# Adding two of the three patterns of a score group in SBUF with an accumulating DMA

## The chip, the cores and the metric

The kernel runs on one core of a Trainium2 chip. The metric is the device time of one execution in microseconds (us), as a median over runs. TensorE multiplies matrices into PSUM, VectorE and ScalarE read PSUM and write SBUF, GpSimd (Pool in the profile) works on SBUF alone and issues DMAs of its own, and SyncE (SP) issues most of the DMAs.

## The reference

Two attention blocks read the same input x of 2048 rows and 512 columns, with 32 heads of 16 columns each. A gate of x mixes their outputs. Block B is the softmax attention with 2048 x 2048 scores per head, and it is most of the work.

```
def _A_ref(x, wqkv, w_phi, wo):          # linear attention
    ...
    phi_q = concatenate([_softmax(pq), _softmax(-pq)])   # same for phi_k
    kv = einsum("bhsf,bhsd->bhfd", phi_k, v);  z = einsum("bhsf->bhf", phi_k)
    o = einsum("bhqf,bhfd->bhqd", phi_q, kv) / (einsum("bhqf,bhf->bhq", phi_q, z)[..., None] + 1e-6)
    return o.reshape(B, S, D) @ wo

def _B_ref(x, wqkv, wo):                 # softmax attention
    ...
    scores = jnp.einsum("bhqd,bhkd->bhqk", q, k) * (Dh ** -0.5)
    p = _softmax(scores, axis=-1)
    o = jnp.einsum("bhqk,bhkd->bhqd", p, v)
    return o.reshape(B, S, D) @ wo

g = _sigmoid((x * gate_w).sum(-1, keepdims=True))
return g * a + (1 - g) * b
```

## The kernel before

The scores of block B are cut into 32 blocks (four heads and 512 queries each), and a block into 64 tiles of 128 keys by 512 queries for one head. That makes 2048 tiles. A tile is made by one score product on TensorE (`qk_mm`, line 994) into one PSUM bank, is turned into exponentials in SBUF in bf16, and is then multiplied with the values into the accumulator bank `psO` (`pv_mm`, line 1136). Column 16 of the values is 1, so the same product gives the softmax sum.

There are two ways from scores to exponentials:

- ScalarE takes two tiles in one exponential (`add_exp`, line 1115; three early pairs are cut in halves). Four such tiles, one for each head, are one value product: four matmuls of 32 columns that lie side by side in the array.
- VectorE takes the tiles counted by `DN` for each block, 756 in all, in groups of four (some of two). It adds a constant to the scores and writes them as 16-bit integers (`add_group`, line 1084; where two tiles' banks allow it, one instruction drains both, line 1074). These bits, read as bf16, are a rough exponential: the first pattern, "t". Pool adds 35 to every 16-bit integer of the group into a second buffer (`shifted`, line 1060, an int64 add over four integers at once): the second pattern, "s". Later Pool adds another 48 in place: the third, "m". TensorE multiplies all three patterns with the same values into `psO` (`add_pvd`), and the errors of the three rough exponentials average out, in the numerator and in the softmax sum alike. So a group has three value products, called terms t, s and m here, and Pool can make m only when term s has been read by TensorE.

The group buffers are taken in turn from free places in SBUF: `Tx`, `Ty`, `Tz`, and weights and buffers that are not needed any more (`WoA`, `WoB`, `oT`, `vA`, `WAT`, `Wp`, `W_B`, `phiQT`); `PHASES` says which ones from which block on. Beside the attention, the other work (projections, block A, the gate, the output product) is laid in between: its products run on TensorE into the seven banks of `psS`, and are drained by VectorE, or for the feature maps of block A by ScalarE (line 1410).

Nothing is scheduled at run time. `Plan.add` collects the operations, and `TABLE` holds one list for each of the five queues ("sp", "act", "pe", "dve", "pool"), written out ahead of time: the order in which each queue issues its operations, the PSUM bank of each filling ("homes"), and which drains are joined in pairs ("pairs"). Each queue is in order, and an operation waits on semaphores for what it depends on. An entry of -1 in the list "pe" is a filler: four matmuls by zeros into `psO` (line 1126). Each DMA semaphore is an engine's wait like any other, so an instruction that waits for a transfer holds up all that stands behind it in its queue. Durations in `Plan.add` are those which the order was laid out with; they have no effect on the chip.

After the last exponential of a block its accumulator is copied out (line 1231), and for the first 30 blocks four small DMAs in a row, issued by SP, gather and spread the softmax sums before VectorE normalises (line 1247).

Of the kernel before, what the change touches and what calls it, by code (L numbers as in the profile page):

```python
# [11 lines left out]
ALU = mybir.AluOpType  # L12
# [18 lines left out]
DN = (16, 24, 18, 24, 26, 26, 26, 20, 22, 22, 24, 18, 26, 24, 20, 26, 30, 22, 24, 26, 22, 24, 30, 26, 18, 22, 36, 18, 24, 24, 32, 16)  # L31
# [31 lines left out]
POOL_ADDS = (0, 203, 69, 203, 69, 203, 69, 195, 69, 235, 69, 203, 69, 195, 69, 202, 69, 218, 69, 203, 101, 203, 68, 195, 69, 219, 65, 203, 71, 203, 69, 203)  # L63
# [5 lines left out]
PAIRING = False  # L69
STEP, RIDE_LAG, EXP_OVH = 0.0, 0.053, 0.051  # L70
# [25 lines left out]
    ),  # L96
    "act": (
# [498 lines left out]
def _build(ctx, nc, A_x, A_wqkv, A_w_phi, A_wo, B_wqkv, B_wo, gate_w, out):  # L596
# [469 lines left out]
    def add_group(g):  # L1066
# [24 lines left out]
        if g is groups[-1]:  # L1091
            last_d1.extend(ops[:len(g["ts"])])
# [570 lines left out]
```

## Time and profile before

| what | value |
|---|---|
| median of three timed runs | 659.58 us (659.51 to 660.69) |
| profiled execution: span from the first to the last instruction | 657.6 us |
| what a timed run has beyond that span | 2.0 us |
| busy: PE / DVE / ACT / POOL | 649.1 / 609.4 / 635.1 / 410.8 us |
| first exponential begins / last one ends | 7.65 us / 649.95 us |
| granted TensorE clock | 1.000 |
| moved by DMA | 30.94 MB |

The profiled execution is known by its span; the page gives no other time for it, so a time is compared with a span by the 2.0 us of the table. A matmul's busy time is its whole way through the array, 0.38 us for 512 columns, while matmuls that lie side by side or follow each other overlap. A PE row of 99% therefore doesn't say that TensorE could do no more. ScalarE's instructions overlap in the same way: the mean length of one is more than the step from one to the next. In the groups, "idle before" is the time in which the engine had nothing running ahead of such an instruction, with the operation that ended it.

### The profile page before, as it was taken

The page shows a single profiled execution, that of the slowest core. Times are in us where ns is not written, and L with a number is a line of the kernel's source. Part 1 is how long each engine was busy: PE and PEld are TensorE (multiplying, and loading weights), DVE is VectorE, ACT ScalarE, POOL GpSimd, SP SyncE. Part 2 cuts the span into 40 slices and gives each one's busy share as a digit, 9 for nine tenths or more (in the row PEclk, how much of TensorE's full clock was granted, in tenths as well). Part 3 has the DMA queues.
Part 4 walks back from the last instruction along what each step waited for, and adds up shares of the span by engine and source line. Part 5 has one row for each costly group of instructions (what it writes and reads, how often), then busy time and mean ns, then how long its engine had stood idle before and what let it go on. Part 6 is the DMA issues. An engine that isn't in the chain of part 4 may idle for free.

```text
span 657.6 us, 20651 instructions
## 1 busy us (share of the span) xinstructions
PE 649.1 (99%) x8820; PEld 227.3 (35%) x8820; DVE 609.4 (93%) x963; ACT 635.1 (97%) x720; POOL 410.8 (62%) x437
## 2 busy tenths in 40 slices
PE   8999999999999999999999999999999999999997
PEld 4333333434333333333233233322333333332333
DVE  6999899999998789999999999999999989999985
ACT  6999999999999999999999999999989999999996
POOL 7575367465665446486467876575867566656853
PEclk9999999999999999999999999999999999999999
DMA  6530101001010000000012431233211633134132
GB/s 131 104 100 12 33 12 27 11 11 19 11 27 10 16 18 8 19 17 14 23 37 47 100 77 33 63 78 68 48 51 35 102 56 83 35 63 103 44 84 48
DMA packets 67947, 30.94 MB, mean 47 GB/s; under 512 B 53208, under 2 KB 62808, under 8 KB 67856
## 3 DMA queue, kind: packets, MB, share of 16 engines
q1 hardware_dynamic: 65840, 28.82, 19.6%
q8 instruction: 69, 1.13, 0.7%
q10 hardware_dynamic: 1632, 0.79, 0.5%
q14 instruction: 22, 0.18, 0.1%
q0 software_dynamic: 384, 0.02, 0.1%
HBM read 7.87 MB, written 8.88 MB: 25 GB/s over the span
## 4 chain that ended last, share of the span: by engine, by line
PE 85%; DVE 12%; ACT 1%; issue 1%; DMA 1%; SPq 0%; DVEq 0%
PE psO L1136 32%; PE psS L994 30%; PE psS L754 15%; DVE Tx_t L1084 3%; PE psS L1417 3%; DVE Ty_t L1084 1%; DVE oT_t L1084 1%; DVE Wp_t L1084 1%; PE psS L842 1%; ACT E_t L1115 1%; DVE Tz_t L1084 1%; PE psS L1514 1%; PE psS L855 1%; PE psO L1126 1%; DMA phiK_t<-in_A_x_dram 1%
## 5 line engine op out<-in xcount | busy, mean ns | idle before, releaser
L1115 ACT ACTIVATE E_t<-psS 128x1024 bf16<-128x1024 f32 x643 | 601.9, 1068 | 11.2 <-PE psS L994 10.3
L994 PE MATMUL psS<-qz_t,kTB_t 32*128 32x512 bf16 (+1 forms) x2054 | 267.5, 383 | 2.8 <-ACT E_t L1104 0.6
L1084 DVE TENSOR_SCALAR Tx_t<-psS 128x512 int16<-128x512 f32 x246 | 163.2, 682 | 10.5 <-PE psS L994 9.4
L994 PEld LDWEIGHTS psS<-qz_t,kTB_t 32*128 32x128 bf16 x2054 | 71.8, 91 | 226.4 <-ACT E_t L1115 102.9
L1136 PE MATMUL psO<-E_t,vaug_t 128*32 128x512 bf16 x1292 | 119.0, 384 | 0.0
L1060 POOL INT64_ADD vA_t<-vA_t x72 | 71.6, 999 | 19.0 <-PE psO L1136 13.7
L1084 DVE TENSOR_SCALAR Ty_t<-psS 128x512 int16<-128x512 f32 x114 | 76.5, 682 | 4.8 <-PE psS L994 4.5
L1060 POOL INT64_ADD Ty_t<-Ty_t x42 | 44.0, 1048 | 18.5 <-PE psO L1136 18.1
L1060 POOL INT64_ADD Ty_t<-Tx_t x29 | 30.1, 1038 | 39.0 <-DVE Tx_t L1084 32.7
L1136 PE MATMUL psO<-vA_t,vaug_t 128*32 128x512 bf16 (+1 forms) x520 | 52.6, 384 | 0.0
L1136 PE MATMUL psO<-Ty_t,vaug_t 128*32 128x512 bf16 x440 | 45.4, 384 | 0.0
L1136 PEld LDWEIGHTS psO<-E_t,vaug_t 128*32 128x32 bf16 x1292 | 30.2, 95 | 39.5 <-issue 28.4
L1084 DVE TENSOR_SCALAR oT_t<-psS 128x512 int16<-128x512 f32 x62 | 41.7, 682 | 1.5 <-PE psS L994 1.0
L1084 DVE TENSOR_SCALAR Tz_t<-psS 128x512 int16<-128x512 f32 x60 | 40.2, 680 | 2.1 <-PE psS L994 1.8
L1060 POOL INT64_ADD vA_t<-Tx_t x22 | 22.7, 1032 | 31.0 <-DVE Tx_t L1084 24.1
L1060 POOL INT64_ADD phiQT_t<-Tx_t x19 | 18.9, 993 | 29.1 <-DVE Tx_t L1084 28.0
L1084 DVE TENSOR_SCALAR vA_t<-psS 128x512 int16<-128x512 f32 x54 | 36.2, 682 | 0.7 <-PE psS L994 0.3
L1084 DVE TENSOR_SCALAR WAT_t<-psS 128x512 int16<-128x512 f32 x52 | 35.2, 682 | 1.4 <-PE psS L994 1.2
L754 PE MATMUL psS<-Wp_t,xT_t 128*32 128x512 bf16 x512 | 35.8, 382 | 0.0
L754 PE MATMUL psS<-xT_t,WB_t 128*32 128x512 bf16 x480 | 34.9, 382 | 0.2
L1084 DVE TENSOR_SCALAR Wp_t<-psS 128x512 int16<-128x512 f32 x50 | 33.8, 683 | 0.9 <-PE psS L994 0.7
L1060 POOL INT64_ADD WoB_t<-oT_t x19 | 19.3, 1016 | 20.7 <-DVE oT_t L1084 16.5
(165 smaller groups left out, 920.1 us busy)
## 6 DMA issues: line engine op xcount, KB each, us to landing
dpq<-EA_t SPq DMA_DIRECT2D x16, 256.0 KB, 2.3
Rb_t<-lr SPq DMA_DIRECT2D x120, 32.0 KB, 1.9
dpo<-kv_t SPq DMA_DIRECT2D x16, 128.0 KB, 1.8
qz_t<-qz_t SPq DMA_DIRECT2D x120, 16.0 KB, 1.8
Tf_t<-Tf_t SPq DMA_DIRECT2D x60, 32.0 KB, 2.0
WB_t<-in_B_wqkv_dram SPq DMA_DIRECT2D x3, 384.0 KB, 3.6
out_dram<-WvA_t SPq DMA_DIRECT2D x8, 128.0 KB, 2.0
out_dram<-WB_t SPq DMA_DIRECT2D x6, 128.0 KB, 2.0
```

What stands on the lines that cost most here:

```text
L754: ins = e.matmul(out[32 * i:32 * i + 32, :], lhsT=lhsT[:, 32 * i:32 * i + 32], rhs=rhs, start=start, stop=stop, tile_position=(0, 32 * i))
L842: mms = [lambda e, ap, i=i, t=t: e.matmul(ap[:, 128 * i:128 * (i + 1)], lhsT=xT[:, t, NQ * c + 128 * i:NQ * c + 128 * (i + 1)], rhs=W_B[:, ...
L855: mms = [lambda e, ap, i=i, t=t: e.matmul(ap[:, 256 * i:256 * (i + 1)], lhsT=xT[:, t, NQ * c + 128 * (2 * hf + i):NQ * c + 128 * (2 * hf + ...
L994: return e.matmul(bank, lhsT=kT_B[32 * i:32 * i + 32, ROW[b // 2] % 2, 128 * kt:128 * (kt + 1)], rhs=qz[32 * i:32 * i + 32, b // 2 % 4, b ...
L1060: op = P.add("pool", P64 + W64 * size, d_prio(g["ts"][0]) - 5.0 + (0.0 if key == "s" else M_LATE), lambda e: e.int64_add(words(dst), words ...
L1084: ops.append(drain(f, mm, "dve", 0.70, d_prio(d), lambda e, ap, q=q: e.tensor_scalar(quarter(tb, q).bitcast(I16), ap, EXPB, 0.0, op0=ALU.a ...
L1115: op = P.add("act", EXP_OVH + 0.4267 * n, 0.0, lambda e: e.activation(Ebuf[:, j // 2 % EPAIRS, 512 * SZ[0] * (j % 2):512 * SZ[0] * (j % 2) ...
L1126: ins = e.matmul((psO if bank is None else bank)[32 * i:32 * i + 32, :], lhsT=zero[:], rhs=xT[:, 0, 0:NQ], start=bank is not None, stop=ba ...
L1136: return e.matmul(psO[32 * i:32 * i + w, :], lhsT=vaug[:, kt, o:o + w], rhs=rhs, start=start, stop=stop, tile_position=(0, 32 * i), skip_g ...
L1417: mms = [lambda e, ap, n=n, f=f: e.matmul(ap[:, 64 * n:64 * n + 64].rearrange("p (s g j) -> p s g j", s=2, j=4), lhsT=ident[:], rhs=es[n][ ...
L1514: mms = [lambda e, ap, g=g: e.matmul(ap[:, 64 * g:64 * g + 64], lhsT=qT(g)[:, 128 * j:128 * (j + 1)], rhs=kzbd[:, g, 0:64], start=True, st ...
```

## The change

Of most groups of VectorE's tiles, the patterns t and s are added together in SBUF, and TensorE multiplies the sum with the values once: two products (t+s, and m) in place of three.

- `SUMS` holds a bit for each group of a block. 158 of the 201 groups are summed. None of blocks 0, 1 and 31 is, nor is the last group (in a few blocks the last two or three) of nearly every other block.
- A new function, `summed`, puts one DMA on Pool's own queue after the group's first add: it reads buffer s and adds it onto buffer t, in bf16, 4 KB in each of 128 partitions (512 KB; two of the groups have 256 KB). Term t waits for its semaphore, since t is now written by the DMA; the add that makes m waits for it too, since it overwrites s. Term s is left out.
- `DN` is changed for single blocks, up or down by 2 or 4, and its sum goes from 756 to 762 tiles: 201 groups in place of 198, and three exponentials of two tiles fewer.
- `TABLE` is laid out anew. Its list "pe" has 2848 entries in place of 3017 (the 23 fillers are gone), "dve" 984 in place of 963, "pool" 597 in place of 433, "act" 690 in place of 693, "sp" 259 as before; 44 pairs of drains are joined in place of 59.

The diff, with the new lists cut out:

```diff
-DN = (16, 24, 18, 24, 26, 26, 26, 20, 22, 22, 24, 18, 26, 24, 20, 26, 30, 22, 24, 26, 22, 24, 30, 26, 18, 22, 36, 18, 24, 24, 32, 16)
+DN = (16, 24, 18, 22, 26, 28, 26, 22, 24, 22, 22, 20, 26, 26, 20, 26, 32, 22, 26, 26, 22, 26, 22, 28, 16, 24, 38, 18, 26, 20, 30, 18)
...
-POOL_ADDS = (0, 203, 69, 203, 69, 203, 69, 195, 69, 235, 69, 203, 69, 195, 69, 202, 69, 218, 69, 203, 101, 203, 68, 195, 69, 219, 65, 203, 71, 203, 69, 203)
...
+SUMS = (0, 0, 15, 31, 63, 63, 63, 31, 31, 31, 31, 15, 63, 63, 15, 15, 127, 31, 63, 63, 63, 63, 31, 63, 7, 31, 511, 15, 127, 31, 127, 0)
...
-            groups.append(dict(ts=mine[n:n + 4], left=len(mine[n:n + 4]), pool=2 * (POOL_ADDS[b] >> n // 4 & 1)))
+            groups.append(dict(ts=mine[n:n + 4], left=len(mine[n:n + 4]), sum=SUMS[b] >> n // 4 & 1))
...
+    def summed(g):
+        size, kind = len(g["ts"]), "a" + g["t"]
+        part = lambda ap: (ap if len(ap.shape) == 3 else ap.rearrange("p (a c) -> p a c", c=512))[:, 0:size, :]
+        dst, src = part(bufs[g["t"]][0]), part(bufs[g["s"]][0])
+        if kind not in chain:
+            chain[kind] = [sem("c_" + kind), 0]
+        chain[kind][1] += 16
+        op = P.add("pool", 0.9, d_prio(g["ts"][0]), lambda e: e.dma_start(dst, src, accum_op=ALU.add), reads=[g["s"]],
+                   writes=[(g["t"], q) for q in range(size)], name=f"sum.{g['n']}", sem=chain[kind][0], lat=5.0)
+        op.semval = chain[kind][1]
+        return op
+
...
+        if g["sum"]:
+            ops.append(summed(g))
         phase_ops[g["ph"]].extend(ops)
...
         term("t", "t")
-        term("s", "s")
+        if not g["sum"]:
+            term("s", "s")
         ops.append(shifted(g, STEPS[1] - STEPS[0], "m"))
         term("m", "s")
```

(`POOL_ADDS` was read into a field that nothing used.)

More of the change, by code (lines that the diff above doesn't have):

```diff
@@ L349 @@
     "homes": (
-        "6705645027467514305342074350243502534104260164320524035135602350263510365015430143620420342604261461024510346013546026140264052310"
-        "5230152035062546025460520625306235102241052450613506452062540264506250426450624045260452452064052065420624502645032650624065235602"
-        "4506420523602520452360542654062405624062405624602560245560425605426504256024606254062554026504620562452406524056204254605240520462"
-        "0642506452602540562054260546256032065426042650420563206245065420253065426043260235602460250423015601350263506230654205230562450624"
@@ L354 @@
-        "6025602506452064250463260244502640241012654062504562406520462563020546202640526045265406250264540265604256034260352405246052064526"
-        "0462506426054260524560423106420602456054205462405620542654065240526404256045260542604256062504265405264062540625046256042605246504"
-        "2605642052402456053260524054205246054256024625064256105362053642045246502405642602305626504260532605320542504260452605426054620456"
-        "2045206425650465204653206523506420542606542064362036520630523230654206425602540654206254602654062540523052643034625042564052604534"
@@ L358 @@
-        "2035013640163561430163015042506245062406452604256042506452605260526025405240652045624562045604250646254065204526045620563263560365"
-        "0240564250436524062405240562405624062365024056254056204562406420546254062305623053620362036042650426503625032560245602460542502465"
-        "0326054625062450635206426402245403601360234502456035461052145042654062504260545216450620452640526045625406240652640524064250325602"
-        "4650320654206530624302456042505246052460264056240526045264026540260542650426052460254602546052460256045256042052540526506230564206"
@@ L362 @@
-        "524054025043560"
+        "6275364520474510365103561043610531653605623065426053260345062406425605264025604256062460546250462560236503206553260436134010346024"
+        "5605425063250623506425042540562046254062460250526042140120410214650230624362043520345106530146214024053104621064210641206402541240"
+        "5124605236024560462034605264024506425602360325063502634032520345016430153015042502451201540260425402164020453104513046314531362502"
+        "3650623025360563046250426506204625045620425065426504206532605426053205624506425024605264052403240134025430164013643015310634203420"
@@ new lines @@
+        "4526052405260436203423065403654103106301564316345101435024360234602410463204602635062364204630425034250364230643053206523204623402"
+        "4650306205325036503205624052460532560243056302524504260546256042065245065204652062540652605206542604256025306243603246023510246124"
+        "0362431206402450632506254062350624505325063420640362403406524046520456204160241260463104315103253015235132051425064256042654023541"
+        "0614320435104361046134102462015423502635602360426046326502306523520345024520615036105361043062340623403245025604236043106340314362"
@@ new lines @@
+        "0436014360134014631354513602513462046013461046103640236410634160530614360153105362036203620653520305623506325062350642064204326430"
+        "1364032643206430104302646302635015305103154530145023520562560625402654062450432345025630245023650346103561034103421640126410260416"
+        "2042604602450254102460126140214612064124062035203506235106350234102614621046120410214240160642164315314035213501206431543052401452"
+        "4056230564206542062530562350630532605235042504526052460532602605240625405624062540265402560425604256042560426062450624506260256052"
@@ L363 @@
+        "062450353106132413"
     ),
```

515 rows, old and new, of the table TABLE are left out of this document.

## The prediction

> **What bounds the kernel now.** I read the busy times first, then the groups and the list of waits, to see who waits for whom.
>
> ```profile
> PE 649.1 (99%) x8820; PEld 227.3 (35%) x8820; DVE 609.4 (93%) x963; ACT 635.1 (97%) x720; POOL 410.8 (62%) x437
> ...
> L1115 ACT ACTIVATE E_t<-psS 128x1024 bf16<-128x1024 f32 x643 | 601.9, 1068 | 11.2 <-PE psS L994 10.3
> L1084 DVE TENSOR_SCALAR Tx_t<-psS 128x512 int16<-128x512 f32 x246 | 163.2, 682 | 10.5 <-PE psS L994 9.4
> L1060 POOL INT64_ADD vA_t<-vA_t x72 | 71.6, 999 | 19.0 <-PE psO L1136 13.7
> ```
> ```profile
> PEld psS L994 <- ACT E_t L1115: 102.9, 258, 0.6
> ...
> ACT E_t L1115 <- PE psS L994: 10.3, 27, 0.8
> ```
>
> Three engines look full, but the waits differ. TensorE waits 102.9 us, in 258 places, for ScalarE to give back a score bank. ScalarE waits 10.3 us for TensorE, in 27 places. So ScalarE sets the pace, and TensorE's 99% is mostly matmuls that overlap. The time lines give the paces:
>
> ```profile
> 7.65 1.56 ACT E_t L1104 x3
> ...
> 422.47 10.28 ACT L1115 ACTIVATE E_t<-psS 128x1024 bf16<-128x1024 f32 x11
> ...
> 643.38 6.57 ACT L1115 ACTIVATE E_t<-psS 128x1024 bf16<-128x1024 f32 x7
> ...
> 650.38 1.25 PE L754 MATMUL psS<-WoA_t,phiK_t 128*32 128x512 bf16 x20
> ```
>
> An exponential costs 10.28 / 11 = 0.935 us. Four side-by-side matmuls of 32 columns cost (1.25 - 0.38) / 4 = 0.22 us, since 20 of them are five sets and the last set's way through takes 0.38 us. The exponentials run from 7.65 to 649.95 us: 642.3 us, in which ScalarE had 11.2 us nothing to do. Only two things can shorten this stretch: fewer exponentials, or fewer of those 11.2 us. VectorE is next:
>
> ```profile
> 300.00:400.00 100.00, 98.96 (x1329) 32.77 (x1321) 96.79 (x158) 99.19 (x113) 69.14 (x68) 1.00 0.22 49
> 400.00:500.00 100.00, 99.34 (x1318) 32.78 (x1316) 95.28 (x151) 98.13 (x112) 66.91 (x69) 1.00 0.22 57
> 500.00:600.00 100.00, 99.86 (x1340) 32.98 (x1340) 96.00 (x155) 98.07 (x111) 62.20 (x63) 1.00 0.32 70
> ```
>
> In these stretches VectorE (the third busy time) is 95 to 97% busy, ScalarE 98 to 99%, and Pool only 62 to 69%.
>
> **The change part by part.** *ScalarE*: three exponentials fewer, 3 x 0.935 = -2.8 us, all of it on the path.
>
> *TensorE*: the 158 sums take 628 matmuls away (156 groups of four tiles, two of two). Six more tiles in groups add 18, six fewer exponential tiles take 6, the 23 fillers take 92. That is 708 matmuls, 177 sets, 177 x 0.22 = 39 us of TensorE's stream. It is off the path wherever TensorE waits for a bank. It can help only where ScalarE waited for TensorE, 10.3 us, and where the drains did. I take a third of the 10.3: -3.4 us, with 0 and -10.3 as the ends. A third is a guess between them: the waits are short (10.3 / 27 = 0.4 us, about two sets), so a set or two less ahead of a score product ends one, but most sets in the queue stay.
>
> *VectorE*:
>
> ```profile
> L1074 DVE TENSOR_SCALAR Tx_t<-psS 128x1024 int16<-128x1024 f32 x21 | 25.6, 1221 | 1.5 <-PE psS L994 1.5
> ```
>
> Six tiles more cost 6 x 0.682 = 4.1 us. Fifteen pairs fewer cost 15 x (2 x 0.682 - 1.221) = 2.1 us. Together +6.2 us, to 615.6. It hides in the 48 us in which VectorE is idle now; were it not hidden, it would cost 6.2 us. I take nothing.
>
> *Pool* gets 158 DMA issues, and its second add waits for the DMA, where it waited for term s on TensorE before. Behind that waiting add stand the first adds and sums of the next groups, and behind these their products. The trace of before has no accumulating DMA. The nearest rows:
>
> ```profile
> 7.97 4.09 POOL L739 DMA_DIRECT2D Wbd_t<-in_A_w_phi_dram  x8 [0.17 <-POOL mask_t L746]
> ...
> L739 POOL DMA_DIRECT2D Wbd_t<-in_A_w_phi_dram x8 | 4.1, 519 | 0.2 <-POOL mask_t L746 0.2
> L735 POOL DMA_DIRECT2D gw_t<-in_gate_w_dram x4 | 2.5, 618 | 0.0
> ```
> ```profile
> dpq<-EA_t SPq DMA_DIRECT2D x16, 256.0 KB, 2.3
> ...
> dpo<-kv_t SPq DMA_DIRECT2D x16, 128.0 KB, 1.8
> qz_t<-qz_t SPq DMA_DIRECT2D x120, 16.0 KB, 1.8
> ...
> WvA_t<-in_A_wqkv_dram SPq DMA_DIRECT2D x1, 512.0 KB, 3.9
> ...
> WoA_t<-in_A_wo_dram SPq DMA_DIRECT2D x1, 512.0 KB, 4.7
> ...
> Wbd_t<-in_A_w_phi_dram POOLq DMA_DIRECT2D x8, 2.0 KB, 2.6
> ...
> gw_t<-in_gate_w_dram POOLq DMA_DIRECT2D x4, 0.2 KB, 3.7
> ```
>
> The issue holds Pool 0.52 to 0.62 us, and 0.17 us passed before the first of them, which waited for Pool's own work, as a sum will for its add; I take 0.54 and 0.17. The landing, counted from the issue's start: 128 KB more cost 0.5 us on SP's queue (1.8 to 2.3), so 512 KB would take 3.3 there. Pool's queue costs 0.8 us more than SP's for small transfers (2.6 against 1.8). That makes 4.1 us for a plain copy. An accumulating one must also read its target. If that costs nothing, 4.1 stays; if the 512 KB are paid a second time (4 x 0.5), it is 6.1. The low end is SP's 3.3, should Pool's 0.8 be the memory that the small rows come from. I take 4.7 us, the row of the whole 512 KB on SP, which lies between: 4.1 to 4.2 us after the issue has ended.
>
> What this means for Pool follows from its list. Full adds cost 1.04 us, adds of two tiles 0.61:
>
> ```profile
> 17.75 1.03 POOL L1060 INT64_ADD Ty_t<-Tx_t  x1 [1.77 <-DVE Tx_t L1074]
> ...
> 646.99 1.04 POOL L1060 INT64_ADD vA_t<-vA_t  x1 [0.54 <-PE psO L1136]
> ```
> ```profile
> L1060 POOL INT64_ADD vA_t<-Tx_t x22: 611/1038/1400, 348.7 to 638.3; - x22
> ...
>   DVE Tx_t L1084: 86.4, 30
>   PE psO L1136: 83.5, 77
> ```
>
> There are 402 adds now (360 full, 42 half): 374 + 26 = 400 us. The 158 issues add 158 x 0.71 = 112 us. Between a sum and its own group's second add the list holds on average 3.2 adds and 1.2 sums (two adds in 25 cases, three in 71, four or more in 56, one in 6). So a landing of about 4.2 us is covered on average, and not in the cases with few. Going down the list with these costs, and stopping at each second add until the landing, Pool stands waiting 45 us in all if the landing comes 4.1 us after the issue's end, 95 us at 5.0, 126 us at 5.5, 157 us at 6.0. The sums are 557, 607, 638 and 669 us. Pool has from its first add at 17.8 us to its last at 648 us, 630 us. At 4.1 us Pool fits, with 73 us left for waits for drains; at 5.5 it doesn't. Of today's waits those for TensorE (83.5 us) go for the summed groups; those for the drains (86.4 us for the largest group of rows) stay in part, where Pool has run out of work. The same list gives TensorE's room: from a summed group's last score product to its term t the median is 11 exponentials, and in 24 of 158 cases 8 or fewer, at 642.3 / 643 = 1.0 us each. The way to the issue's end takes 0.38 + 0.68 + 1.04 + 0.71 = 2.8 us, so the tight cases leave 5.2 us for the landing and all queueing. At 4.1 us nothing waits but where queues are full. I put +1.0 us for that.
>
> *DMA engines*: 158 sums carry 82 MB where all DMAs carry 31 MB now.
>
> ```profile
> DMA packets 67947, 30.94 MB, mean 47 GB/s; under 512 B 53208, under 2 KB 62808, under 8 KB 67856
> ...
> q8 instruction: 69, 1.13, 0.7%
> ```
>
> At this row's share per MB (the largest packets of any queue here) 82 MB are 51% of 16 engines' time. SP's small transfers, the four in a row of the normalisation above all, get slower by part of a sum's 2 us (4 x 0.5). No VectorE instruction waits for a DMA of that chain in the list of waits today, so there is cover. I take nothing more than the +1.0 above; without that cover, four transfers late by 1 us in each of 15 chains would be up to 60 us.
>
> The sum: 657.6 - 2.8 - 3.4 + 1.0 = 652.4 us of span. The median of the runs shown is 2.0 us above the span of this execution, so **654.4 us**. Its own range runs from -2.8 - 10.3 (646.5) to no help from TensorE and +3 for landings (660 with the 2.0); I call it 647 to 658, since beyond 658.3 (0.2%, about what a measurement can tell from no change) it is another case.
>
> **The rivals.**
>
> *The Pool round trip* (slower). The landing is nearer to 6.1 than to 4.7 us, and Pool's queue becomes the bound: every first add stands behind a second add that waits for a DMA. It decides from about 5 us after the issue's end, where list and drain waits together reach the 630 us. At 5.56 (the upper bound, 6.1 - 0.54) the list alone needs 641 us, 11 more than there are; with a fourth of the 86.4 us of drain waits left, the span is 652.4 + 11 + 21 = 684, the time 686 us. For it: nothing here shows that the second read is free. Against it: even SP's 512 KB out of another memory land in 4.7.
>
> *Late sums one by one* (slower). Pool keeps up, but transfers queue behind each other and land 1 to 2 us late. If one in eight of the 158 terms t is late by 1 us, TensorE stands 20 us, and since ScalarE is only a bank or two ahead I let half reach it: +10 us, 664 us. For it: in-order queues, and 24 tight cases. Against it: the 39 us which TensorE gets back.
>
> *No change.* TensorE was not the bound, so its 39 us become longer waits for ScalarE; the 2.8 us saved on ScalarE come back as VectorE, with 6.2 us more, gives banks back later. 659 us.
>
> *Descriptors held up by VectorE* (slower). Pool would have to wait for the end of a drain at each issue: +0.68 us, 158 x 0.68 = +107 us on Pool's queue, 557 + 107 = 664 us of list for 630, so 652.4 + 34 + 2 = 688 us. The row above speaks against it: with VectorE at 95 to 97%, the adds keep a median of 1038 ns, and Pool doesn't stand still beside VectorE. The Trainium skill, "SBUF — State Buffer", section "Summary: rules for kernel authors", says not to hide a Pool-issued DMA under a VectorE instruction in a fast mode, since the writing of descriptors is starved; it names tensor_scalar, the drains' operation, among those that can. By that rule this case would come; the row of the adds doesn't agree with it so far, the drains here read PSUM, and no run here shows an issue beside a drain.
>
> **How the numbers follow.** The forecast gets 0.48, the round trip 0.25, late sums 0.15, no change 0.08, held-up descriptors 0.04. Faster by over 0.2% is the forecast's 0.48; slower 0.25 + 0.15 + 0.04 = 0.44; the same 0.08. The range goes from the forecast's 647 through late sums and the round trip at its upper bound to 686; beyond lie the rest of the round trip, the held-up descriptors and the forecast's own tails, less than 2 in 10.
>
> **What would show it.** Pool's issue row with 158 entries near 0.54 us, and its landing near 4.7 us: right; above 5.5, the round trip. Waits of Pool's adds for a DMA near 45 us in all: right; above 100, wrong. The exponentials' idle time under 11 us, released by TensorE: right; 20 us or more, ahead of value products that wait for DMAs: late sums. Issues of 1.2 us: held-up descriptors. The value products' row should lose 610 matmuls. Slower than 658.3 us makes the forecast wrong.

## The result: slower by a quarter

The changed kernel takes 824.47 us (median of four runs, 818.07 to 828.9) against 660.02 us (659.51 to 660.69) for the kernel before on the same chip: a ratio of 1.2488, 95% interval 1.2423 to 1.2553. The forecast was 654.4 us, the range 647 to 686: the sign was wrong, and the time lies 138 us above the range's end. The profiled execution has a span of 826.9 us, 169.3 more than before. One execution each of the runs e1, e2, e10, e11 and e18 below lies more than 1.5% above the fastest of its kernel and is left out of the times given for them, while the expectations, written earlier, count it (677 us for e1).

Lines of the page after: busy times, the granted clock and the DMA engines' share in 40 slices, Pool's DMA queue, and three groups.

```profile
PE 722.7 (87%) x8112; PEld 226.4 (27%) x8112; DVE 642.0 (78%) x984; ACT 649.5 (79%) x717; POOL 568.8 (69%) x601
...
PEclk9996899889999899998988568698799787977979
DMA  7373566577776655766879879889679876899952
...
q0 software_dynamic: 34400, 82.34, 56.5%
...
L1142 ACT ACTIVATE E_t<-psS 128x1024 bf16<-128x1024 f32 x640 | 613.4, 1033 | 162.2 <-PE psS L1007 158.8
...
L1073 POOL INT64_ADD vA_t<-vA_t x72 | 84.7, 1182 | 15.3 <-PE psO L1163 5.4
...
L1275 DVE TENSOR_TENSOR oT_t<-Tf_t,Rb_t 128x512 bf16<-128x512 f32 x15 | 18.5, 1236 | 28.0 <-DMA Rb_t<-lr 28.0
```

The matmuls fell by 708, as the prediction counted. But the exponentials, which set the pace before with 11.2 us of idle time, now stand idle for 162.2 us, nearly all of it waiting for score products. That row holds 151 of the 169 us between the two profiled executions. No engine takes the place of ScalarE: none is above 87%. VectorE's quotient (L1275), which never waited before, waits 28.0 us for the last transfer of the normalisation.

The list of waits after, then the rows of the sum's line: length of an issue in ns (least, median, most), who waited for a sum, and the time from issue to landing:

```profile
ACT E_t L1142 <- PE psS L1007: 158.8, 150, 8.8
...
PEld psS L1007 <- ACT E_t L1142: 86.4, 196, 1.9
...
DVE oT_t L1275 <- DMA Rb_t<-lr: 28.0, 10, 8.3
```
```profile
L1086 POOL DMA_DIRECT2D Tx_t<-Ty_t x23: 864/877/1205, 48.9 to 769.7; - x23
...
L1086 POOL DMA_DIRECT2D Ty_t<-WB_t x6: 1301/1319/1821, 404.3 to 788.1; - x6
...
  PEld psO L1163: 28.3, 22
  PE psO L1163: 19.5, 17
  POOL Ty_t L1073: 12.5, 8
...
DMA to landing us min/median/max: 4.5/5.6/9.7
```

An issue holds Pool 0.88 us, or 1.3 where a side is one of the weight buffers whose rows lie in 1 KB pieces. The landing has a median of 5.6 us. SP's transfers became slower too (median us to landing, last column; before they were 1.8, 2.0, 1.8 and 1.6):

```profile
qz_t<-qz_t SPq DMA_DIRECT2D x120, 16.0 KB, 2.9
Tf_t<-Tf_t SPq DMA_DIRECT2D x60, 32.0 KB, 3.8
...
Lq_t<-ld SPq DMA_DIRECT2D x30, 8.0 KB, 3.2
...
lr<-rd_t SPq DMA_DIRECT2D x15, 16.0 KB, 2.8
```

One stall in the time line shows how a late sum reaches ScalarE (start, length, engine, line, and in brackets the idle time ahead):

```profile
55.79 0.87 POOL L1086 DMA_DIRECT2D oT_t<-WoB_t  x1 [0.30 <-POOL WoB_t L1073]
...
63.28 0.62 PE L1163 MATMUL psO<-oT_t,vaug_t 128*32 128x512 bf16 x4 [2.30 <-DMA oT_t<-WoB_t]
...
63.32 1.04 POOL L1073 INT64_ADD WoB_t<-WoB_t  x1 [2.96 <-DMA oT_t<-WoB_t]
...
64.93 1.02 ACT L1142 ACTIVATE E_t<-psS 128x1024 bf16<-128x1024 f32 x1 [2.93 <-PE psS L1007]
```

The sum issued at 55.79 us let its readers go some 7.5 us later. Its term t stood ahead of the next score products in TensorE's queue, so the exponential came 2.93 us late. It is natural to read the whole loss as many such stalls. The runs put only a small part of it there.

### The profile page after: what moved, and what is told of

Read it like the earlier page. It is cut to its first block, busy times and chain, and to the rows that moved or that the text cites. A ratio compares the mean times of both kernels' runs of the same rounds, so it can differ in the third digit from the quotient of the medians.

```text
span 826.9 us, 19603 instructions
## 1 busy us (share of the span) xinstructions
PE 722.7 (87%) x8112; PEld 226.4 (27%) x8112; DVE 642.0 (78%) x984; ACT 649.5 (79%) x717; POOL 568.8 (69%) x601
## 3 DMA queue, kind: packets, MB, share of 16 engines
q0 software_dynamic: 34400, 82.34, 56.5%
## 4 chain that ended last, share of the span: by engine, by line
PE 32%; DMA 23%; DVE 16%; POOL 11%; SPq 9%; issue 7%; ACT 2%; ACTq 0%; DVEq 0%; POOLq 0%
PE psS L1007 12%; PE psO L1163 11%; PE psS L767 6%; DMA ld<-Tf_t 4%; SPq L1272 4%; DVE Tx_t L1109 4%; DMA Rb_t<-lr 3%; DMA lr<-rd_t 3%; SPq L1517 2%; DMA Lq_t<-ld 2%; POOL vA_t L1073 2%; ACT E_t L1142 2%; POOL Ty_t L1073 2%; DVE Tz_t L1109 1%; SPq L1266 1%
## 5 line engine op out<-in xcount | busy, mean ns | idle before, releaser
L1142 ACT ACTIVATE E_t<-psS 128x1024 bf16<-128x1024 f32 x640 | 613.4, 1033 | 162.2 <-PE psS L1007 158.8
L1007 PE MATMUL psS<-qz_t,kTB_t 32*128 32x512 bf16 (+1 forms) x2054 | 320.0, 425 | 38.9 <-DVE Ty_t L1109 8.6
L1109 DVE TENSOR_SCALAR Tx_t<-psS 128x512 int16<-128x512 f32 x260 | 169.9, 683 | 38.0 <-PE psS L1007 36.5
L1163 PE MATMUL psO<-E_t,vaug_t 128*32 128x512 bf16 x1286 | 140.4, 428 | 10.1 <-DVE Tf_t L1259 9.4
L1073 POOL INT64_ADD vA_t<-vA_t x72 | 84.7, 1182 | 15.3 <-PE psO L1163 5.4
L767 PE MATMUL psS<-Wp_t,xT_t 128*32 128x512 bf16 x512 | 45.0, 420 | 0.0
L1163 PE MATMUL psO<-Ty_t,vaug_t 128*32 128x512 bf16 x308 | 38.3, 438 | 7.1 <-POOL Ty_t L1073 4.6
L1163 PE MATMUL psO<-vA_t,vaug_t 128*32 128x512 bf16 (+1 forms) x330 | 39.9, 453 | 2.8 <-POOL vA_t L1073 2.8
L1163 PE MATMUL psO<-Tx_t,vaug_t 128*32 128x512 bf16 x290 | 34.1, 432 | 9.4 <-DMA Tx_t<-vA_t 4.0
L1275 DVE TENSOR_TENSOR oT_t<-Tf_t,Rb_t 128x512 bf16<-128x512 f32 x15 | 18.5, 1236 | 28.0 <-DMA Rb_t<-lr 28.0
```

What stands on the lines that cost most here:

```text
L767: ins = e.matmul(out[32 * i:32 * i + 32, :], lhsT=lhsT[:, 32 * i:32 * i + 32], rhs=rhs, start=start, stop=stop, tile_position=(0, 32 * i))
L1007: return e.matmul(bank, lhsT=kT_B[32 * i:32 * i + 32, ROW[b // 2] % 2, 128 * kt:128 * (kt + 1)], rhs=qz[32 * i:32 * i + 32, b // 2 % 4, b ...
L1073: op = P.add("pool", P64 + W64 * size, d_prio(g["ts"][0]) - 5.0 + (0.0 if key == "s" else M_LATE), lambda e: e.int64_add(words(dst), words ...
L1109: ops.append(drain(f, mm, "dve", 0.70, d_prio(d), lambda e, ap, q=q: e.tensor_scalar(quarter(tb, q).bitcast(I16), ap, EXPB, 0.0, op0=ALU.a ...
L1142: op = P.add("act", EXP_OVH + 0.4267 * n, 0.0, lambda e: e.activation(Ebuf[:, j // 2 % EPAIRS, 512 * SZ[0] * (j % 2):512 * SZ[0] * (j % 2) ...
L1163: return e.matmul(psO[32 * i:32 * i + w, :], lhsT=vaug[:, kt, o:o + w], rhs=rhs, start=start, stop=stop, tile_position=(0, 32 * i), skip_g ...
```

## The experiments

All of them change the one operation that issues a sum, unless said otherwise:

```
op = P.add("pool", 0.9, ..., lambda e: e.dma_start(dst, src, accum_op=ALU.add), reads=[g["s"]],
           writes=[(g["t"], q) for q in range(size)], ..., lat=5.0)
```

The theories: the *landing* is waited for (the prediction's round trip); the *load* on the DMA engines slows everything that uses them; *Pool's time* for the issues; the *new order* itself. In short:

| in the place of each sum | waited for | new order | old order |
|---|---|---|---|
| nothing (in the new order a tiny memset) | - | 676.0 us | 659.5 us |
| Pool's shift repeated | yes | 695.2 us | |
| the same and a shorter add | yes | 749.9 us | |
| 16 KB accumulated | yes / no | 722.7 / 724.4 us | - / 709.2 us |
| 256 KB accumulated | yes | 740.9 us | |
| 512 KB accumulated, every second sum | yes | 749.5 us | |
| 512 KB copied | yes / no | 729.6 / 724.8 us | |
| 512 KB accumulated | yes / no | 824.5 / 804.1 us | - / 761.8 us |

The transfers without a wait add or copy into device memory and leave the sums out; of those that add, the first eight are plain copies, which fill the eight places there.

**The order and the fewer products, without transfers.**

```
-  e.dma_start(dst, src, accum_op=ALU.add)
+  e.memset(spare[:, k:k + 1], 0.0)
```

> The same order, with a one-column memset on GpSimd in the place of each of the 158 transfers, so that s is never added to t (pattern s is left out of the result for the summed groups). Theory A, the transfers load the DMA engines and so delay both themselves and SyncE's small transfers: without them 648 to 660 us and a granted clock back at 1.00. Theory B, the order itself is at fault (fewer products and no fillers let TensorE's clock fall, pairs are gone): still above 720 us, clock still under 0.95.

675.99 us (670.86 to 678.5), ratio 1.0207 [1.0159, 1.0254].

```profile
PE 655.7 (97%) x8112; PEld 223.0 (33%) x8112; DVE 620.4 (92%) x984; ACT 637.4 (94%) x717; POOL 430.3 (64%) x601
```
```profile
300.00:400.00 100.00, 96.93 (x1112) 30.37 (x1109) 90.64 (x142) 89.76 (x100) 63.76 (x84) 0.89 0.18 44
```

Both theories missed: most of the loss does hang on the transfers, but with none at all the new order is some 16 us slower than the old (10 to 17 by the interval). The new order stands here for all that e1 keeps: the new lists, two products in place of three, and term t's wait for its turn in Pool's list. The second fence is a stretch from the table of stretches (PE, PEld, VectorE, ScalarE, Pool busy, clock, DMA share): ScalarE, busy 99.19 us of this stretch before, is busy 89.76, and the clock is 0.89. Is it the clock of a TensorE with less to do? The next run keeps the memset and gives back the third product:

```
-  term("m", "s")
+  term("m", *(("s", "s") if g["sum"] else ("s",)))
```

> Changed order, a tiny GpSimd memset in the place of each sum (as in the run without transfers, 677 us), and each summed group's last value product made twice over, so that a group again has three products. Theory 'the order itself': the 17 us above the kernel before come from how the new lists interleave; the third product adds 39 us of TensorE stream to lists laid out for two, so the time is 677 to 715 us. Theory 'a less busy TensorE loses its clock': the clock returns from 0.977 to that of before and the time falls to 658 to 666 us.

697.11 us (695.73 to 701.76), ratio 1.0564 [1.0515, 1.0614]. The clock came back (0.99 in the profiled execution, from 0.977) and the time rose by 21 us. So a TensorE with more to do doesn't win the 16 us back. Whether the clock has a part in them stays open, since this run also lengthens TensorE's stream, by 157 sets or some 35 us at 0.22; e1's own executions go from 670.86 us at a clock of 0.992 to 678.5 at 0.977, and even the first is 11 us above the old kernel. The run shows as well that in the new order, without transfers, a third product has a price. And the reverse, fewer matmuls in the old order:

```
   work = [(d["t"], quarter(bufs[g[k]][0], q)) for k in keys for q, d in enumerate(g["ts"])]
+  if name == "s":
+      work = work[:1]
```

> The kernel before in its own order, with three of the four matmuls of each group's second value product left out (no transfers, nothing on GpSimd): what the fewer matmuls of the change are worth by themselves. Theory 'ScalarE bounds, as its 97 % says': at most the waits for TensorE go, 652 to 659 us. Theory 'TensorE bounds': some 480 matmuls of about 62 ns each are 30 us, 628 to 640 us. A result above 661 us would say that a thinner TensorE is slower by itself.

659.47 us against 659.46 us, ratio 0.9998 [0.9988, 1.0007].

```profile
PE 647.9 (98%) x8262; PEld 226.0 (34%) x8262; DVE 608.8 (93%) x963; ACT 634.7 (96%) x720; POOL 410.8 (62%) x437
```
```profile
ACT E_t L1115 <- PE psS L994: 11.1, 28, 0.9
```

558 matmuls fewer change nothing: PE's busy time moves by 1.2 us, and ScalarE's waits for TensorE stay at 11.1 us (10.3 before). But the run doesn't take a product out of TensorE's stream. It leaves out three of four matmuls that lie side by side, and the fourth takes almost as long alone. The same place before and in this run (start, length):

```profile
311.20 0.39 PE L1136 MATMUL psO<-oT_t,vaug_t 128*32 128x512 bf16 x4
311.52 0.61 PE L994 MATMUL psS<-qz_t,kTB_t 32*128 32x512 bf16 x4
```
```profile
311.04 0.38 PE L1136 MATMUL psO<-oT_t,vaug_t 128*32 128x512 bf16 x1
311.36 0.61 PE L994 MATMUL psS<-qz_t,kTB_t 32*128 32x512 bf16 x4
```

The next score product starts 0.32 us later in both. Over all such places the median is 0.322 us behind four matmuls (222 places before) and 0.312 behind one (130 places here). So this run doesn't tell what the 39 us of stream that the change saves are worth in the old order; no run does.

**Load or wait.** First a plain copy of the same size, with and without the wait for it, then an accumulating one without.

```
e2_load:     e.dma_start(far[k, ...], xT[...])          # into device memory, nobody waits
e3_copy:     e.dma_start(dst, src)                      # no accum_op, same waits
e8_accload:  e.dma_start(far[k % 8, ...], xT[...], accum_op=ALU.add)   # nobody waits
```

> As before this one, but each sum's place in GpSimd's queue issues a plain 512 KB transfer from x in SBUF to HBM, for which no product and no add waits (pattern s is left out of the result). Theory A1, the load on the DMA engines acts through the other transfers (the normalisation's, the gathers of block A): 690 to 760 us. Theory A2, the wait for the sums' own landing is what costs: under 670 us.

724.76 us, from a single execution.

> The same transfers on the same buffers and with the same waits, but as plain copies without the add (t is overwritten by s). If reading the target is a second transfer's worth of engine time, the engines' time for each sum falls from about 3.0 to 2.0 us or less, the landing from 5.6 to about 4.5 us, and the time to 700 to 750 us. If the add costs nothing, the time stays at 815 to 830 us.

729.57 us (725.33 and 733.8), ratio 1.1058 [1.0982, 1.1134]. A copy takes 30.5% of the DMA engines in all and lands in 3.4 us at the median, and waiting for it costs 5 us, less than its two executions differ by.

> Changed order; in the place of each sum GpSimd issues an accumulating transfer of the same 512 KB into device memory that no instruction waits for (the sums are left out). The plain copy that nobody waited for gave 730.6 us. Theory 'load': the accumulating transfers hold the DMA engines about twice as long as copies and slow everything else there, so the time is 780 to 830 us with nobody waiting. Theory 'landing waited for': without the wait the time stays at 725 to 745 us, and the rest up to 824 is the wait for the sum by the next shift and by the products.

804.13 us (798.3 and 809.97), ratio 1.2169 [1.2061, 1.2277]. Nobody waits for a sum, and yet the time is only 20 us below the changed kernel's (798 to 810 us against 818 to 829). From the page and the list of waits of this run:

```profile
q0 software_dynamic: 23136, 82.34, 58.9%
...
L1147 ACT ACTIVATE E_t<-psS 128x1024 bf16<-128x1024 f32 x640 | 609.4, 1037 | 144.2 <-PE psS L1009 140.9
```
```profile
DVE oT_t L1280 <- DMA Rb_t<-lr: 40.2, 8, 15.7
```

So the landing that is waited for, the prediction's chief rival, is some 20 us of the 164. (The unwaited transfers go to device memory and not to SBUF; they hold the DMA engines about as long, 58.9% of 808.1 us over 158, or 3.01 us each.) An accumulating transfer holds the DMA engines twice as long as a copy: 56.5% of 826.9 us over 158 sums is 2.96 us of all 16 engines for each, 30.5% of 723.3 us for the copies is 1.40.

How does the load act? The normalisation's transfers are the first suspect. Its gathers and spreads go to spare device memory, and reciprocal and quotient read constants. SP issues them as before:

```
-  e.dma_start(Lq[:, par, :], ld[par]...)   [("ld", par)], [("Lq", par)]
+  e.dma_start(farq[par], ld[par]...)       [("ld", par)], [("farq", par)]
   (the same for the moves mg and rb)
```

> The changed kernel, but the softmax normalisation's four small transfers write into spare HBM, and VectorE's reciprocal and product read constants, so that they wait for none of these transfers (the result is not normalised; all transfers still run). Theory A1, the slow small transfers ahead of VectorE carry most of the loss: 700 to 750 us. Theory A2, the sums' own landing carries it: 800 us or more.

798.46 us (794.5 and 802.41) with the sums waited for, 26 us less than the changed kernel.

> Changed order; the accumulating transfers go to device memory with no instruction waiting for them (the sums are left out), and no instruction waits for the normalisation's small transfers either (quotients are taken from constants). Waiting for the normalisation alone, the load gave 804 us. Theory 'the load acts through the normalisation chain': 685 to 715 us. Theory 'the load also acts elsewhere' (other transfers, GpSimd's issues, the engines themselves): above 760 us.

757.01 us, from a single execution; so once more, with more of them:

> The version with 512 KB accumulating transfers that nobody waits for and a normalisation that nobody waits for, again, since its two executions lay 33 us apart (757 and 790). Theory 'the load acts mostly through the normalisation chain': below 745 us. Theory 'mostly elsewhere': above 765 us, less than half of the 80 us between 724 and 804. Between the two: about half and half.

769.26 us (765.94 to 770.9), ratio 1.1643 [1.1595, 1.1691]. VectorE's waits for the normalisation carry 804 - 769 = 35 us of the 80 that the bytes add (724 to 804), or 47 by e10: about half. But only VectorE was freed. SP's queue is in order, and it still stands for the links of the chain (SPq is SP's queue; the kernel before, then e18):

```profile
SPq L1235 <- DMA ld<-Tf_t: 13.6, 12, 1.5
...
SPq L1244 <- DMA lr<-rd_t: 7.4, 6, 1.5
```
```profile
SPq L1271 <- DMA ld<-Tf_t: 80.0, 25, 11.9
SPq L1280 <- DMA lr<-rd_t: 42.7, 14, 8.3
```
```profile
PE psS L1537 <- DMA phiQT_t<-dpq: 22.1, 1, 22.1
```

So the rest may still come from the chain, through the transfers behind it in SP's queue. The other candidate is block A's transposes and shuffles, slower themselves: in e18 TensorE stands for them 22.1 us (the last line, one wait) and twice 9.1 us more, in e10 17.1 us for `dpo`. The two weren't separated.

**How the loss grows with the bytes.**

```
e6_half:  part = ...[:, 0:2, :]        # 256 KB of a sum's 512
e7_alt:   if k % 2: memset instead     # every second sum
e9_tiny:  part = ...[:, 0:1, 0:64]     # 16 KB
```

> As the changed kernel, but each sum moves and accumulates only the first half of its tile (256 KB of 512 KB), with the same issues and waits. Theory 'engine time': an accumulating transfer of 256 KB takes about 1.5 us of the DMA engines, what the copy of 512 KB took (1.4), so the time is that of the copy version, 725 to 740 us, with landings near 3.2 us. Theory 'accumulation as such' (each accumulating transfer is a slow round trip, whatever its size): landings stay above 4.5 us and the time above 780.

740.94 us (738.75 and 743.13), ratio 1.1213 [1.1162, 1.1263]; landings at a median of 3.8 us, 0.4 later than whole copies; Pool's queue takes 34.2% of the engines. That is 1 us above what "engine time" allowed and far from "accumulation as such".

> As the changed kernel, but only every second sum is a transfer; the others are a tiny memset. Half of the accumulated bytes, in transfers of full size. Theory 'engine time': with half of the bytes the engines are as loaded as in the version with half-size transfers, and the time is within 10 us of that one. Theory 'landing waited for': each sum still takes over 4 us from its issue and costs its (824 - 677) / 158 = 0.93 us, so 79 of them give 677 + 74 = 750 us, clearly above the half-size version if that one lands in 3.2 us.

749.53 us (744.15 and 754.92), ratio 1.1343 [1.1243, 1.1443]. Within 10 us of the half-size version and on the price of "landing waited for": the two theories gave nearly the same number, and this run doesn't tell them apart. It does suggest that the bytes alone don't set the loss. If 79 issues cost half of what 158 cost (48 us, below), the same bytes cost 50 us here, in transfers of full size, and 17 in twice as many of half the size.

> As the changed kernel, but each sum accumulates only 64 of its 2048 columns (16 KB): the same 158 issues on GpSimd, the same waits for the landing, almost no bytes. Theory 'load': what the transfers take of the DMA engines is the cost, so with 1/32 of the bytes the time falls to 677 to 695 us (677 without any transfer, plus issues of about 0.9 us in GpSimd's free time). Theory 'round trip': issue and landing at the shortest (about 2 us) still stand in GpSimd's list and ahead of the products; then the time stays above 710 us.

722.7 us (720.28 and 725.12), ratio 1.0939 [1.0841, 1.1037]. With 1/32 of the bytes, 47 of the 148 us above 676 remain. Issue, or round trip?

```
e14_tinyload:  e.dma_start(far[k % 8, :, 0:64], xT[:, 0, 0:64], accum_op=ALU.add)   # nobody waits
```

> Changed order; in the place of each sum an accumulating transfer of 16 KB into device memory that no instruction waits for (the sums are left out). Theory 'the issue costs, not the wait': as with the wait, 715 to 730 us. Theory 'the wait for the landing costs': 677 to 695 us.

724.37 us (723.4 and 725.34), ratio 1.0986 [1.0964, 1.1008]: as with the wait. The issue costs, not the wait, and not the load either: SP's transfers of 16 and 32 KB land in 1.8 and 2.0 us here, as in the kernel before.

**Pool's time.** The same without any transfer:

```
e13_pooltime:   e.int64_add(words(s), words(t), STEPS[0] * ...)     # the shift ahead, again
e17_pooltime2:  the same, and ahead of it an add of 512 columns into a spare tile
```

> Changed order without any transfer; in the place of each sum GpSimd repeats the shift that stands ahead of it (the same values again, an add of 1.0 to 1.2 us), so that GpSimd's list is as full as with the issues of 0.9 to 1.3 us. The version with 16 KB transfers took 723 us, the one with a tiny memset 677. Theory 'GpSimd's time': 710 to 735 us. Theory 'the transfer itself (descriptors, landing)': 677 to 692 us.

695.16 us (694.84 and 695.47), ratio 1.0543 [1.0522, 1.0564]. Between the theories, 19 of the 48 us.

> As the version in which GpSimd repeats a shift in the place of each sum (695 us), with a second, shorter add of 512 columns ahead of it (0.3 to 0.4 us, into a spare tile): about 1.4 us of GpSimd's list per sum, what an issue of 0.91 us, the 0.29 us ahead of it and the 0.2 us by which the shift behind it is longer make together. No transfer. Theory 'GpSimd's time is all of it': 715 to 730 us, as with the 16 KB transfers (723). Theory 'something else of the issue' (VectorE's longer quotients, descriptors): 697 to 710 us.

749.85 us (744.57 and 755.13), ratio 1.1362 [1.1267, 1.1457]. More than the issues cost, and no byte is moved. How much of Pool's list each takes is read from its time lines; here e9, then e13, then e17:

```profile
300.20 1.36 POOL L1073 INT64_ADD WoA_t<-Tz_t  x1
301.85 0.88 POOL L1086 DMA_DIRECT2D Tz_t<-WoA_t  x1 [0.30 <-POOL WoA_t L1073]
302.45 1.36 POOL L1073 INT64_ADD Ty_t<-Ty_t  x1
```
```profile
299.92 1.04 POOL L1075 INT64_ADD WoB_t<-oT_t  x1
301.05 1.04 POOL L1086 INT64_ADD WoB_t<-oT_t  x1
302.07 1.04 POOL L1075 INT64_ADD phiQT_t<-phiQT_t  x1
```
```profile
302.23 1.04 POOL L1075 INT64_ADD Ty_t<-Tx_t  x1 [0.44 <-DVE Tx_t L1110]
303.37 0.40 POOL L1087 INT64_ADD spare_t<-Tx_t  x1
303.74 1.04 POOL L1088 INT64_ADD Ty_t<-Tx_t  x1
304.76 1.04 POOL L1075 INT64_ADD phiQT_t<-Tx_t  x1
```

Adds start 1.02 us apart. Around an issue it is 302.45 - 300.20 = 2.25, so a sum takes 1.23 us of Pool's list (its 0.88 overlaps the next add, but 0.30 stand ahead of it, and the add before it must have ended). The repeated shift takes 302.07 - 299.92 - 1.02 = 1.13, the longer version 304.76 - 302.23 - 1.02 = 1.51; the medians over each run are 1.22, 1.13 and 1.51. Time against list: 0 gives 676, 1.13 gives 695, 1.51 gives 750 us, so Pool is near its limit there and each further tenth costs some 14 us (55 / 0.38). At 1.23 the line between the last two gives 710, the line through the first two 697; where the curve bends wasn't measured. So Pool's time explains 21 to 34 of the issues' 48 us, and 14 to 27 stay open (VectorE's longer quotients, below, may be in them).

**The old order under the same load.** Behind the first shift of 158 groups the kernel before gets the same unwaited transfers; it still has its three products, and nothing reads what is moved.

> The kernel before in its own order, and behind the first shift of 158 groups an accumulating transfer of 16 KB into device memory that no instruction waits for. Theory 'an issue costs wherever it stands': 660 + 46 = 706, so 695 to 720 us. Theory 'only the new order feels it': 659 to 675 us.

709.24 us (706.41 and 712.08), ratio 1.0757 [1.0707, 1.0806]: 50 us for the issues, 48 in the new order.

> The kernel before, in its own order and with its three products, and beside it, behind the first shift of 158 groups, an accumulating transfer of 512 KB into device memory that no instruction waits for. Theory 'load': it costs what it cost in the new order (804 - 677 = 127 us), so 760 to 800 us. Theory 'the new order is what gives way': the old order bears the same load with less than half of that, below 720 us.

761.78 us, from a single execution: 101 us above the kernel before, where the new order lost 128. The issues strike the old order as hard; the bytes cost it 53 us (709 to 762), the new one 80. So the new order isn't what gives way, though part of the load's price may be its own. Whether some other order would escape isn't shown by two of them.

> As the changed kernel, but each sum accumulates only 64 of its 2048 columns (16 KB), and the last product of each summed group is made twice over (three products per group). Against the run with three products and no transfers (697 us) it shows what the 158 issues and shortest round trips cost where TensorE is as full as in the kernel before. Theory 'issues are free': within 10 us of 697. Theory 'issue and round trip cost': above 720.

The kernel that ran under this label accumulated the whole 512 KB of each sum, not the 64 columns that its expectation names; so it is the changed kernel with three products per group, and is to be held against 824 us. It took 829.98 us (828.86 and 831.09). The third product back, 628 matmuls, costs some 6 us, while the clock rises from 0.872 to 0.911. So in the changed kernel TensorE's stream is hardly what limits, and a higher clock doesn't bring the time back.

## Why the prediction was wrong, point by point

In the order of its steps, with the parts of the 164 us as one path through the runs gives them (e1, e14, e8, the changed kernel): 16 for the order, 48 for the issues, 80 for the bytes on the DMA engines, 20 for waiting for the landing. The executions of e8 and of the changed kernel each spread over some 11 us, so the last two are known to about that.

- *ScalarE, -2.8 us.* The three exponentials did go (x640 for x643). With every transfer gone, the time still rose. Whether the 2.8 are inside the +16 can't be seen.
- *TensorE, -3.4 us of a possible -10.3.* Not settled. The 708 matmuls did go, but e16 left the stream almost as long as it was and so doesn't price them. In the new order without transfers ScalarE's waits for TensorE are 23.0 us, more than the 10.3 of before. Nor did the saving come back as longer waits for ScalarE, as the rival *no change* had it: TensorE's list has 99.4 us of them there, 102.9 before.
- *VectorE, +6.2 us hidden.* Not tested by itself; VectorE's busy time without transfers is 620.4 us where 615.6 was forecast.
- *The new order.* The prediction priced what was added and removed and gave the order itself nothing. It costs some 16 us with nothing to transfer.
- *Pool's issue, 0.54 + 0.17 us.* The first mis-sized term. Those rows were plain transfers, and for plain copies the length was right: 0.546 us in the copy version. An accumulating issue lasts 0.88, and 1.3 for 1 KB pieces, with 0.30 ahead. In the list that is 1.23 us, not 0.71: 158 x 1.23 = 194 us instead of 112. By the prediction's own sum, 400 + 194 + 45 = 639 us of list where it had 630. So the issues alone bring Pool past that limit, and the runs give them 48 us, of which 21 to 34 are Pool's time. No rival priced that for its own reason: *held-up descriptors* asked for about the same time per issue, but nothing points to VectorE. In the copy version, with VectorE 88% busy, the contiguous issues were 0.545 to 0.556 us at the median, and none lasted over 0.584.
- *Landing, 4.7 us, bounds 3.3 to 6.1.* Measured 5.6, and 3.4 for a copy where 4.1 was reckoned. The doubled time on the DMA engines (2.96 against 1.40 us) fits the upper bound's reason, a second read that is paid; the landing itself was measured only beside the other sums. Pool's adds waited 52 us in all for sums (the rows of the sum's line for Pool added up), near the 45 forecast, and TensorE 47.8 us in 39 places, which is the rival *late sums*. But taking all of these waits away brings some 20 us, where that rival had 10. The sign "above 5.5: the round trip" came true and pointed to the wrong cause: that rival gave 686 us by Pool's waits for landings, and most of the way to 824 is there without them.
- *DMA engines, "I take nothing more".* The step that failed by most: 80 us. The prediction took 51% of 16 engines from a queue of plain transfers, 335 us in all; the sums took 467 us (56.5% of 826.9). Then it said that since no VectorE instruction waits for the normalisation's chain, there is cover. The cover was thinner than four slowed transfers: the quotient waited 28.0 us. Its bound without cover, 60 us for that chain, held for VectorE's waits (35 to 47 measured). The other 33 to 45 us it hadn't listed. It had looked at VectorE's waits alone, while SP, whose queue the chain shares with block A's transfers, waited 13.6 and 7.4 us for `ld` and `lr` already before, and 51.9 and 28.2 in the changed kernel. Which path carries those 33 to 45 us stays open.

The rows that could have warned were there: SP's landings of 1.8 us, of which the kernel has a few hundred, and a DMA share of 0.06 to 0.32 in the stretches; the changed kernel's is 0.51 to 0.87.

How steeply the cost rises shows in three versions with the same issues and waits: with 16, 256 and 512 KB in a sum, Pool's queue takes 7.5, 34.2 and 56.5% of the DMA engines, and the time is 723, 741 and 824 us. The first half of the bytes costs 18 us, the second 84.

## What to carry to other kernels

A DMA that accumulates isn't a copy with the addition for nothing: here it held the DMA engines twice as long (2.96 against 1.40 us) and its issue held Pool 1.6 times as long (0.88 against 0.55). When a product is to be traded for transfers, first take the product out alone, with all of its matmuls: if the time doesn't move, there is nothing to pay with. Leaving out some of the matmuls that lie side by side, as here, takes almost nothing off the stream and answers nothing. And price the queue that issues by the distance between its neighbours' starts, and the load by an unwaited transfer of the same kind in the old kernel; each is one run. Look for cover in the list of waits of the queue that issues a chain, too, and not only in that of the engine that uses its result.

## What the runs showed of the hardware

The landing of an accumulating transfer from Pool was 2.3 us at the median for 16 KB, 3.8 for 256 KB and 5.6 for 512 KB, and 3.4 for a plain copy of 512 KB:

```profile
DMA to landing us min/median/max: 2.0/2.3/4.3
```
```profile
DMA to landing us min/median/max: 3.3/3.8/6.0
```
```profile
DMA to landing us min/median/max: 2.8/3.4/6.5
```

(16 KB, 256 KB, and the copy.) The Trainium skill, "DMA: Bandwidth & Descriptors", section "Anatomy of one DMA — SWDGE (gpsimd) path", gives about 2.0 us and the bytes at 436 GB/s for a DMA of this kind, from which an estimate of 3.2 us follows for 512 KB: the copy agrees with its 3.4 us, the accumulating one doesn't with its 5.6.

VectorE's quotient reads two tiles of SBUF; it took 716 ns in the mean in the kernel before, and 1372 with 16 KB sums:

```profile
L1247 DVE TENSOR_TENSOR oT_t<-Tf_t,Rb_t 128x512 bf16<-128x512 f32 x15 | 10.7, 716 | 0.0
```
```profile
L1275 DVE TENSOR_TENSOR oT_t<-Tf_t,Rb_t 128x512 bf16<-128x512 f32 x15 | 20.6, 1372 | 2.5 <-DMA Rb_t<-lr 2.5
```

The drains, which read PSUM, kept their 681 to 684 ns. The mean hides two kinds of quotient. One beside an issue of Pool's, from e8, and one beside adds, from e14:

```profile
208.39 0.87 POOL L1091 DMA_DIRECT2D far<-xT_t  x1 [0.30 <-POOL oT_t L1075]
208.45 0.69 DVE L1280 TENSOR_TENSOR oT_t<-Tf_t,Rb_t 128x512 bf16<-128x512 f32 x1 [3.26 <-DMA Rb_t<-lr]
```
```profile
689.68 4.34 DVE L1280 TENSOR_TENSOR oT_t<-Tf_t,Rb_t 128x512 bf16<-128x512 f32 x1
...
690.10 1.35 POOL L1075 INT64_ADD vA_t<-Tx_t  x1
691.12 1.34 POOL L1075 INT64_ADD WB_t<-WB_t  x1
```

The Trainium skill, "SBUF — State Buffer", section "Who interferes with whom", says that a VectorE instruction with two SBUF inputs contends with a Pool instruction that reads SBUF. The rows agree, since the adds read SBUF. In the traces of all runs and both kernels, every one of the 137 quotients over 0.72 us overlaps an add, 74 of them no issue at all, while the 18 that stand beside issues alone took 0.68 to 0.69 us. So an issue doesn't lengthen a quotient; an add can. Why the runs with more issues have more of the long ones wasn't followed.
